# RG-LRU scan with mixture of experts on one core: all zero fills in a new fixed order of the main part, and the experts one after the other

## The chip, the cores and the metric

The kernel runs on one core of one Trainium2 chip. The metric is the device time of one execution in microseconds, the median of three runs. Five instruction queues work side by side: TensorE (PE, with its weight loads as PEld), VectorE (DVE), ScalarE (ACT), GpSimd (POOL), and SyncE (SP), which in this kernel does nothing but issue DMA transfers. Each queue runs its instructions in order. The instruction at its head waits until what it needs has been signalled.

## What is computed

```python
a_t = exp(8 * sigmoid(r_gate) * log(clip(sigmoid(a_param))))   # decay, per token and channel
u_t = sqrt(max(1 - a_t**2, 1e-6)) * sigmoid(i_gate) * x
h_t = a_t * h_(t-1) + u_t          # scan over 5056 tokens, 4 sequences, 256 channels
logits = h @ w_gate                # 20224 tokens, 8 experts
out = 0                            # (20224, 256)
for e in range(8):                 # at most 80 tokens of each expert, those of highest gate
    out[tok] = gate[tok] * (relu(h[tok] @ w1[e]) @ w2[e])
```

All but some 640 of the 20224 rows of the output are zero. They have to be written all the same, 20.7 MB; the three inputs are 62.1 MB together and the experts' weights 16.8 MB.

## The kernel before

**Main part** (lines 32 to 287). The 20224 tokens are cut into 22 units. Unit 0 and unit 1 are halves of 512 tokens, units 2 to 19 have 1024 tokens, unit 20 has 512 and unit 21 has 256. The order of all instructions of this part is written out by hand in the string ORDER, and each word of it becomes instructions on one queue. For unit u:

- `ru@s`, `iu@s`, `xu@s`: SP issues the load of r_gate, i_gate or x into slot s of the big tile Y (1 MB for a full unit)
- `Tu`: ACT takes tanh of r (line 117). `Au.h`: PE transposes it for channel half h (line 123). `Eu.h`: ACT takes exp and writes the decay into the state slot of the unit (line 126)
- `Qu`: POOL squares the decay (line 129). `Su.m`: ACT takes the square root for units u to u+m-1 (line 133); this needs another function table than tanh and exp, so every S group has a table load ahead of it and one behind it
- `Iu`: ACT takes tanh of i (line 137). `Uu`: POOL multiplies by x (line 140)
- `Bu.h`: PE transposes and adds (lines 147 and 148). `Nu.h`: DVE multiplies by the root (line 151). `Yu.h`: DVE scans (line 161)
- `lu`: PE computes the logits (line 237). `cs.k`: step k of the selection for chain s of units. `t`: an early search for the largest gates (line 272)
- `Z`: SP writes zeros to rows of the output. As long as no decay of the last pair (units 20 and 21) has been issued, one Z is one wide fill of 512 tokens (line 209, 0.5 MB in packets of 4 KB). After that, one Z is two narrow fills of 256 tokens (line 215, 0.25 MB each, packets of 1 KB)

The zeros of a wide fill are read from the state slot of the last pair, `Y[:, 19, 0]`. `E20.0` writes the first decay of unit 20 into the same place, so it can't start before every wide fill has been done.

Slots are shared. A load waits on SP until the last reader of what stood in its slot is done, and everything behind it on SP waits too. State slot p is free for streams until pair p gets its state, so there are fewer slots for streams towards the end.

**Selection** (lines 290 to 445). SP issues the weights of experts 0 and 1 (lines 300 and 303) and then `FILLS` = 11 narrow fills. DVE, POOL, ACT and PE find the 80 tokens of each expert. `keep_warm` (line 348) issues 13 and then 10 matmuls that nobody reads. `front` (line 514) fetches the column numbers of experts 0 and 1 into registers (`fetch`, line 497) and copies those columns of the state into XG (`copies`, lines 505 and 506): 32 by ACT, 24 by POOL and 24 by DVE for each expert.

**Experts** (line 531). The six fills that are left are issued first. For each expert, `first` is the product with w1 in two halves of 32 matmuls (line 546), `relu` empties a half (ACT half 0, DVE half 1), `second` is the product with w2 in two halves of 32 (line 556), `take` (ACT), `turn` (PE), `weigh` (DVE) and `scatter` (POOL, an indirect DMA) bring the result out. Weights have two buffers: w1 of expert e+2 is loaded when `first(e, 1)` is done, w2 of e+2 by halves when `second(e, half)` is done. The loop is staggered: the two halves of `first(k+1)` stand between the halves of `second(k)`.

Of the kernel before, what the change touches and what calls it, by code (L numbers as in the profile page):

```python
# [36 lines left out]
i8@13 N4.1 T8 B5.0 x8@18 E7.0 N5.0 I6 A7.1 Y4.1 i9@11 l3 E7.1 U6 Y5.0 T9 A8.0 B5.1 E8.0 i10@20 N5.1 I7 A8.1 Q7 Z B6.0 r11@17 Y5.1 E8.1 T10
A9.0 N6.0 U7 l4 E9.0 Y6.0 I8 A9.1 B6.1 c0.1 E9.1 Q8 B7.0 r12@24 N6.1 S7.2 x9@16 x10@12 Y6.1 l5 U8 c0.2 A10.0 N7.0 B7.1 Y7.0 E10.0 x11@22 Z
Q9 N7.1 I9 A10.1 i11@15 B8.0 Y7.1 E10.1 l6 T11 Q10 N8.0 c0.3 T12 A11.0 Y8.0 B8.1 c0.4 U9 E11.0 c0.5 r13@18 I10 i12@13 A11.1 N8.1 l7 E11.1
c0.6 r14@23 B9.0 Q11 S9.3 Y8.1 c0.7 A12.0 B9.1 N9.0 U10 c0.8 l8 Y9.0 i13@16 N9.1 I11 B10.0 x12@21 Y9.1 E12.0 U11 N10.0 T13 A12.1 c1.1 B10.1  # L40
Y10.0 E12.1 r15@20 I12 A13.0 Q12 Z N10.1 B11.0 E13.0 x13@14 Y10.1 c1.2 T14 A13.1 U12 N11.0 B11.1 I13 Y11.0 l9 E13.1 i14@22 x14@15 T15 N11.1
Q13 B12.0 c1.3 i15@17 S12.2 l10 Y11.1 U13 B12.1 N12.0 Y12.0 A14.0 r16@21 Z c1.4 I14 N12.1 B13.0 x15@24 Y12.1 E14.0 U14 I15 A14.1 N13.0
B13.1 E14.1 Y13.0 T16 i16@16 A15.0 Q14 l11 N13.1 E15.0 B14.0 c1.5 x16@18 S14.1 Z U15 Y13.1 A15.1 N14.0 B14.1 E15.1 Y14.0 r17@22 I16 Q15
A16.0 Z l12 N14.1 E16.0 B15.0 i17@23 Y14.1 S15.1 Z U16 A16.1 c1.6 B15.1 N15.0 l13 r18@24 E16.1 Y15.0 x17@17 T17 Q16 c1.7 Z N15.1 I17 A17.0
# [592 lines left out]
```

## Time and profile before

| what | value |
|---|---|
| median of 3 runs | 304.96 us (304.64 to 305.4) |
| the profiled execution, its own time | 304.55 us |
| its span, first to last instruction | 302.8 us |
| time outside the span in that execution | 1.75 us |
| busy share of the span: PE, DVE, ACT, POOL | 77%, 69%, 75%, 67% |
| moved by DMA | 100.95 MB, 333 GB/s over the span |
| mean granted clock of TensorE | 0.928 of full speed |

The time is the span and a constant around it. A busy share is an average over parts with different limits, so the tables by stretches are read first, then the timelines of single engines. "DMA share" in a stretch is the mean busy share of the 16 DMA engines; it can come out a little above 1. Releasers of waits are inferred from semaphores.

### The profile page before, as it was taken

Reading aid. Unit: us, or ns where it says so; the run is one execution under the profiler, and the core shown is the slowest. Engines: PE = TensorE matmul, PEld = TensorE weight load, DVE = VectorE, ACT = ScalarE, POOL = GpSimd, SP = SyncE. Lnnn points to the kernel's source line nnn. Section 1 sums busy time; section 2 is a strip of 40 time slices with the busy share of each in tenths; the row PEclk is TensorE's granted clock in tenths of the full one; section 3 lists DMA queues with packets and bytes.
Section 4 is the critical chain, followed back from the end, with each engine's and each line's share of the span. In section 5 each row is a group of like instructions: output and inputs, shape, how many; then the busy total and the mean of one; then the engine's idle time right before and its main releaser. Section 6 shows DMA issues by size and latency. Waiting matters only on the chain.

```text
span 302.8 us, 9258 instructions
## 1 busy us (share of the span) xinstructions
PE 231.9 (77%) x3422; PEld 204.9 (68%) x3422; DVE 209.5 (69%) x435; ACT 226.7 (75%) x441; POOL 202.2 (67%) x289
## 2 busy tenths in 40 slices
PE   1466489989989979979887976736739858999972
PEld 0355488878978878868776965635517658888761
...
GB/s 232 410 409 409 411 350 384 394 411 371 323 398 351 351 355 233 417 379 309 293 416 412 251 327 418 337 228 368 346 309 378 373 193 179 353 375 353 357 138 32
DMA packets 42436, 100.95 MB, mean 333 GB/s; under 512 B 3216, under 2 KB 22544, under 8 KB 42384
## 3 DMA queue, kind: packets, MB, share of 16 engines
...
HBM read 78.91 MB, written 21.36 MB: 331 GB/s over the span
## 4 chain that ended last, share of the span: by engine, by line
PE 13%; issue 11%; ACT 10%; DMA 10%; POOL 6%; DVE 6%; SPq 3%; POOLq 2%; ACTq 1%; DVEq 0%
DMA Y<-in_i_gate_dram 6%; POOL Y L506 3%; PE pd L348 3%; DMA Y<-in_r_gate_dram 3%; SPq L215 3%; ACT Y L505 3%; PE pu L147 2%; PE pu L148 2%; DVE Y L161 2%; ACT Y L133 2%; POOLq L499 2%; POOL Y L140 2%; ACT Y L126 1%; PE po L556 1%; ACT L133 1%
## 5 line engine op out<-in xcount | busy, mean ns | idle before, releaser
L140 POOL TENSOR_TENSOR Y<-Y 128x2048 f32<-128x2048 f32 (+2 forms) x22 | 90.7, 4122 | 27.2 <-ACT Y L137 18.0
L161 DVE TENSOR_TENSOR_SCAN Y<-Y,pu 128x1024 f32<-128x1024 f32 (+8 forms) x50 | 93.2, 1881 | 0.8
L129 POOL TENSOR_TENSOR Y<-Y 128x2048 f32<-128x2048 f32 (+2 forms) x22 | 71.6, 3258 | 21.2 <-ACT Y L126 12.6
L147 PE MATMUL pu<-ident,Y 128*128 128x128 f32 x316 | 78.3, 290 | 9.6 <-DVE Y L161 8.3
L151 DVE SCALAR_TENSOR_TENSOR pu<-Y,pu 128x1024 f32<-128x1024 f32 (+2 forms) x44 | 48.4, 1109 | 46.8 <-ACT Y L133 39.2
L148 PE MATMUL pu<-ident,Y 128*128 128x128 f32 x316 | 76.9, 287 | 5.0 <-POOL Y L140 4.9
L123 PE MATMUL pr<-ident,Y 128*128 128x128 f32 x316 | 51.3, 311 | 32.7 <-ACT Y L126 23.2
L123 PEld LDWEIGHTS pr<-ident,Y 128*128 128x128 f32 x316 | 40.5, 159 | 40.7 <-ACT Y L126 30.4
L126 ACT ACTIVATE Y<-pr,tiny 128x1024 f32<-128x1024 f32 (+2 forms) x44 | 49.0, 1113 | 14.7 <-PE pr L123 8.8
L147 PEld LDWEIGHTS pu<-ident,Y 128*128 128x128 f32 x316 | 47.2, 149 | 14.0 <-DVE Y L161 9.8
L148 PEld LDWEIGHTS pu<-ident,Y 128*128 128x128 f32 x316 | 47.2, 149 | 6.8 <-POOL Y L140 6.6
L137 ACT ACTIVATE Y<-Y 128x2048 f32<-128x2048 f32 (+2 forms) x22 | 38.1, 1733 | 3.6 <-DMA Y<-in_i_gate_dram 3.6
L237 PE MATMUL pl<-Y 128*32 128x64 f32 (+2 forms) x1344 | 39.2, 280 | 0.8 <-DVE Y L161 0.8
L117 ACT ACTIVATE Y<-Y 128x2048 f32<-128x2048 f32 (+2 forms) x22 | 38.0, 1731 | 0.7 <-DMA Y<-in_r_gate_dram 0.7
L133 ACT ACTIVATE Y<-Y 128x2048 f32<-128x2048 f32 (+2 forms) x22 | 37.3, 1733 | 1.2 <-POOL Y L129 1.1
L237 PEld LDWEIGHTS pl<-Y 128*32 128x32 f32 x1344 | 33.8, 125 | 4.5 <-issue 3.3
L505 ACT COPY Y<-Y 128x2 f32 x256 | 25.7, 192 | 12.5 <-POOL Y L506 7.6
L506 POOL COPY Y<-Y 128x2 f32 x192 | 24.6, 196 | 14.0 <-issue 7.2
L546 PE MATMUL ph<-Y 128*64 128x80 f32 x512 | 25.1, 249 | 8.5 <-ACT Y L505 5.3
L546 PEld LDWEIGHTS ph<-Y 128*64 128x64 f32 x512 | 22.3, 149 | 10.2 <-issue 5.6
L506 DVE COPY Y<-Y 128x2 f32 x192 | 20.9, 179 | 7.9 <-issue 7.9
L556 PE MATMUL po<-rows,Y 128*64 128x80 f32 x512 | 22.4, 241 | 0.0
...
## 6 DMA issues: line engine op xcount, KB each, us to landing
...
```

The lines of the kernel that those rows point to most:

```text
L123: nc.tensor.transpose(pr[:, c0:min(n, g + 512):nb], rr[:, at:at + P], ident)
L126: nc.scalar.activation(state(u, h), prs.pop((u, h))[:, :UNITS[u][2]], AF.Exp, scale=L[:, h:h + 1], bias=L[:, h:h + 1])
L129: nc.gpsimd.tensor_tensor(halves('r', u), a, a, op=ALU.mult)
L133: nc.scalar.activation(q, q, AF.Sqrt, scale=-0.25, bias=0.25)
L140: nc.gpsimd.tensor_tensor(i, i, flat('x', u), op=ALU.mult)
L147: nc.tensor.matmul(cols, xx[:, at:at + P], ident, start=True, stop=False, is_transpose=True)
L148: nc.tensor.matmul(cols, ii[:, at:at + P], ident, start=False, stop=True, is_transpose=True)
L151: nc.vector.scalar_tensor_tensor(pu, halves('r', u)[:, h], 0.5e-3, pu, op0=ALU.max, op1=ALU.mult)
L161: nc.vector.tensor_tensor_scan(y[:, s0:s1], y[:, s0:s1], q[:, s0:s1], init, op0=ALU.mult, op1=ALU.add)
L237: nc.tensor.matmul(pl[32 * j:32 * j + 32, s % 2, c0:c0 + n // NR], gates(h, b), Y[:, p, h, o + 4 * j + b:o + n:NR], start=(b == 0 and h == ...
L506: else: eng.tensor_copy(dst, src)
L546: nc.tensor.matmul(ph[j:j + P // 2, c % (FC // 2)], w1v(e)[:, h, c * P + j:c * P + j + P // 2], XG[:, e % 4, h], start=(h == 0), stop=(h = ...
```

## The change

1. `FILLS` and the two calls of `zero_fill` with it are gone. ORDER has 39 Z instead of 31: 23 wide fills (18 before) and 16 pairs of narrow ones (13 before), which is 78 of the 79 pieces of 256 tokens; one narrow fill follows behind the weights of experts 0 and 1. Before, 17 narrow fills followed there.
2. ORDER is new. The streams of the first and of the last units go to other slots and stand in another order. There are 11 S groups instead of 12.
3. `WARM` goes from (13, 10) to (13, 19).
4. The experts' loop runs expert by expert: both halves of `first`, then both halves of `second`.

```diff
-WARM = (13, 10)
+WARM = (13, 19)
-FILLS = 11
...
-r0@20 r1@20 r2@21 r3@22 T0 i0@23 A0.0 x0@24 w E0.0 T1 A0.1 r4@18 E0.1 T2 Q0 A1.0 i1@23 E1.0 r5@17 A1.1 E1.1 T3 A2.0 x1@24 E2.0 i2@16 I0
-A2.1 U0 E2.1 x2@15 I1 A3.0 Q1 B0.0 E3.0 i3@14 T4 A3.1 Q2 x3@13 E3.1 T5 A4.0 Q3 r6@12 E4.0 I2 A4.1 i4@11 B0.1 U1 E4.1 S0.4 r7@10 U2 N0.0
...
-c2.4 S17.1 c2.5 B17.1 U18 c2.6 A18.0 i19@23 Z c2.7 l16 N17.0 Z Z E18.0 N17.1 Z T19 c2.8 A18.1 c3.1 x19@22 Y17.0 c3.2 E18.1 I19 Z Q18 c3.3
-B18.0 Y17.1 c3.4 A19.0 S18.1 c3.5 B18.1 c3.6 l17 r20@20 N18.0 Z U19 Z E19.0 c3.7 N18.1 A19.1 Y18.0 i20@24 r21@20 E19.1 Z Z T20 c3.8 Q19
-Y18.1 A20.0 B19.0 E20.0 S19.1 t B19.1 A20.1 x20@22 Z Z x21@22 T21 Z E20.1 i21@24 Z I20 Q20 A21.0 l18 N19.0 E21.0 Z N19.1 U20 A21.1 E21.1 Z
-Y19.0 Z Q21 S20.2 Y19.1 B20.0 Z Z I21 N20.0 B20.1 U21 c4.1 Y20.0 c4.2 Z l19 N20.1 Z c4.3 B21.0 Y20.1 c4.4 Z c4.5 B21.1 l20 N21.0 Z N21.1
...
+r0@20 i0@21 r1@20 r2@22 r3@23 T0 A0.0 x0@24 w E0.0 T1 A0.1 i1@21 E0.1 r4@18 I0 Q0 A1.0 E1.0 T2 A1.1 i2@17 E1.1 T3 Q1 A2.0 x1@24 i3@16 E2.0
+U0 I1 A2.1 E2.1 x2@15 B0.0 T4 Q2 A3.0 B0.1 i4@14 E3.0 I2 A3.1 U1 x3@13 E3.1 Q3 S0.4 A4.0 r5@12 N0.0 N0.1 x4@11 U2 Y0.0 Y0.1 B1.0 r6@10 N1.0
...
+Y16.1 B17.0 c2.5 B17.1 c2.6 A18.0 I18 i19@23 N17.0 Z c2.7 l16 Z Z E18.0 U18 Y17.0 T19 A18.1 c3.1 c2.8 E18.1 N17.1 c3.2 I19 c3.3 Q18 x19@20
+B18.0 Z Y17.1 Z c3.4 Z S18.1 c3.5 B18.1 c3.6 U19 r20@24 r21@24 N18.0 c3.7 A19.0 N18.1 E19.0 Y18.0 x20@22 A19.1 Z x21@22 E19.1 Z Z c3.8
+B19.0 Z Y18.1 T20 Q19 T21 A20.0 E20.0 t B19.1 S19.1 A20.1 i20@20 l17 i21@20 Z Z Z Z E20.1 Q20 A21.0 N19.0 Z E21.0 I20 A21.1 N19.1 l18 Z I21
+U20 Y19.0 E21.1 Z Q21 S20.2 Z Y19.1 B20.0 U21 Z N20.0 Z c4.1 Y20.0 c4.2 B20.1 Z c4.3 B21.0 N20.1 l19 c4.4 Z N21.0 Y20.1 Z c4.5 B21.1 l20
...
-    zero_fill(FILLS)
+    zero_fill(-(-N // ZERO_TOKENS))
...
-        for k in 'APV': fetch(k, 0); copies(k, 0)
+        for k in 'APV': fetch(k, 0)
+        for k in 'APV': copies(k, 0)
...
-        nz[0] = filled
-        zero_fill(-(-N // ZERO_TOKENS))
...
-        first(0, 0); relu(0, 0); first(0, 1)
         for k in range(E):
-            e1, e2 = (k + 1 if k + 1 < E else None), (k + 2 if k + 2 < E else None)
-            if e2 is not None:
-                for q in 'APV': fetch(q, e2)
-            relu(k, 1)
-            if k >= 1: take(k - 1)
-            if e2 is not None:
-                copies('A', e2, 0, nA // 2); copies('P', e2); copies('V', e2)
-            if e1 is not None: first(e1, 0)
-            if k >= 1: turn(k - 1)
-            second(k, 0)
-            if e1 is not None: relu(e1, 0)
-            if e2 is not None: copies('A', e2, nA // 2)
-            if e1 is not None: first(e1, 1)
-            if k >= 1: weigh(k - 1); scatter(k - 1)
-            second(k, 1)
+            g = k + 2
+            if k: take(k - 1)
+            if 0 < k < E - 1: copies('A', g - 1, 16, 24)
+            first(k, 0); relu(k, 0)
+            if 0 < k < E - 1: copies('A', g - 1, 24); copies('V', g - 1, 20)
+            first(k, 1); relu(k, 1)
+            if k: turn(k - 1); weigh(k - 1)
+            if g < E:
+                for q in 'APV': fetch(q, g)
+                copies('A', g, 0, 16); copies('V', g, 0, 20); copies('P', g)
+            if k: scatter(k - 1)
+            second(k, 0); second(k, 1)
```

## Rows read from the trace of the kernel before

**Rows 1.** Timeline of SP from 188 us: start, duration, line, what it issues, count.
```profile
188.84 0.95 SPq L209 DMA_DIRECT2D out_dram<-Y  x2
...
204.55 15.44 SPq L215 DMA_DIRECT2D out_dram<-Y  x20
220.10 1.21 SPq L300 DMA_DIRECT2D Y<-in_moe_w_dram  x2
```

**Rows 2.** Stretches: busy time and instructions of each engine, granted clock, DMA share, GB/s.
```profile
0.00:220.00 220.00, 170.04 (x2310) 150.82 (x2310) 167.15 (x171) 191.32 (x144) 162.99 (x66) 0.95 0.95 355
4.00:44.00 40.00, 23.25 (x104) 20.02 (x105) 5.90 (x11) 33.78 (x27) 23.59 (x8) 0.87 1.03 409
72.00:128.00 56.00, 51.36 (x767) 46.20 (x766) 51.99 (x46) 55.33 (x38) 54.91 (x15) 1.00 0.93 345
128.00:152.00 24.00, 20.94 (x273) 18.87 (x272) 22.87 (x20) 23.49 (x18) 22.40 (x6) 1.00 0.97 331
164.00:181.00 17.00, 13.71 (x204) 12.59 (x205) 16.06 (x20) 14.71 (x11) 14.12 (x4) 0.90 0.87 303
181.00:195.00 14.00, 8.90 (x112) 7.76 (x111) 12.23 (x15) 10.01 (x8) 8.41 (x4) 0.85 1.02 415
```

**Rows 3.** Waits of ACT from 4 to 34 us: total, times, longest.
```profile
ACT Y L126 <- PE pr L123: 5.9, 8, 1.2
```

**Rows 4.** Wide fills issued from 128 to 152 us: count, duration of the issue, first and last start.
```profile
L209 SPq DMA_DIRECT2D out_dram<-Y x4: 455/459/754, 129.3 to 148.2; - x4
```

**Rows 5.** Timeline around 190 us: POOL U19, PE A20.0, ACT E20.0; idle before in brackets.
```profile
188.75 4.51 POOL L140 TENSOR_TENSOR Y<-Y 128x2048 f32<-128x2048 f32 x1 [3.14 <-DMA Y<-in_x_dram]
...
192.54 1.11 PE L123 MATMUL pr<-ident,Y 128*128 128x128 f32 x4 [2.24 <-ACT Y L117]
...
198.30 0.78 ACT L126 ACTIVATE Y<-pr,tiny 128x512 f32<-128x512 f32 x1 [5.81 <-PE pu L147]
```

**Rows 6.** Timeline of ACT at one S group: the table load and the root behind it.
```profile
139.71 1.28 ACT L133 ACT_TABLE_LOAD   x1
141.01 1.92 ACT L133 ACTIVATE Y<-Y 128x2048 f32<-128x2048 f32 x1
```

**Rows 7.** Timeline of the tail of the main part: T21, E20.1, I20, E21.1, S20.2, N20.0.
```profile
203.61 0.63 ACT L117 ACTIVATE Y<-Y 128x512 f32<-128x512 f32 x1
204.15 0.76 ACT L126 ACTIVATE Y<-pr,tiny 128x512 f32<-128x512 f32 x1
204.81 1.05 ACT L137 ACTIVATE Y<-Y 128x1024 f32<-128x1024 f32 x1
...
208.07 0.56 ACT L126 ACTIVATE Y<-pr,tiny 128x256 f32<-128x256 f32 x1 [1.76 <-PE pr L123]
...
209.95 1.58 ACT L133 ACTIVATE Y<-Y 128x1024 f32<-128x1024 f32 x2
...
211.04 0.70 DVE L151 SCALAR_TENSOR_TENSOR pu<-Y,pu 128x512 f32<-128x512 f32 x1 [1.86 <-PE pu L147]
```

**Rows 8.** Timeline of PE: keep_warm, first(0), second(0, 0), the last second.
```profile
237.24 4.58 PE L348 MATMUL pd<-Y,ident 128*128 128x256 f32 x20
244.97 4.08 PE L546 MATMUL ph<-Y 128*64 128x80 f32 x64 [3.15 <-ACT Y L505]
...
252.43 2.41 PE L556 MATMUL po<-rows,Y 128*64 128x80 f32 x32
...
294.20 2.44 PE L556 MATMUL po<-rows,Y 128*64 128x80 f32 x64
```

**Rows 9.** Timeline of ACT in the experts: relu(0, 0), then take(0) and take(1).
```profile
251.35 0.44 ACT L562 ACTIVATE rows<-ph 128x320 f32<-128x320 f32 x1 [0.29 <-issue]
...
258.51 0.29 ACT L563 COPY Y<-po 128x160 f32<-128x160 f32 x1 [1.54 <-DVE rows L561]
...
263.91 0.29 ACT L563 COPY Y<-po 128x160 f32<-128x160 f32 x1 [1.77 <-PE po L556]
```

**Rows 10.** Waits of PE from 244 to 303 us, of the first product for weights.
```profile
PE ph L546 <- DMA Y<-in_moe_w_dram: 1.6, 3, 0.7
```

More of the change, by code (lines that the diff above doesn't have):

```diff
@@ L32 @@
 ORDER = """
-r0@20 r1@20 r2@21 r3@22 T0 i0@23 A0.0 x0@24 w E0.0 T1 A0.1 r4@18 E0.1 T2 Q0 A1.0 i1@23 E1.0 r5@17 A1.1 E1.1 T3 A2.0 x1@24 E2.0 i2@16 I0
-A2.1 U0 E2.1 x2@15 I1 A3.0 Q1 B0.0 E3.0 i3@14 T4 A3.1 Q2 x3@13 E3.1 T5 A4.0 Q3 r6@12 E4.0 I2 A4.1 i4@11 B0.1 U1 E4.1 S0.4 r7@10 U2 N0.0
-N0.1 x4@9 Y0.0 Y0.1 B1.0 Q4 i5@8 A5.0 N1.0 B1.1 Y1.0 r8@23 I3 N1.1 B2.0 Y1.1 E5.0 U3 N2.0 x5@20 T6 A5.1 Y2.0 B2.1 E5.1 i6@24 N2.1 I4 A6.0
-Q5 B3.0 Y2.1 r9@21 E6.0 T7 A6.1 N3.0 U4 B3.1 x6@16 I5 Y3.0 l1 E6.1 i7@15 N3.1 Q6 S4.3 B4.0 Y3.1 x7@22 A7.0 l2 N4.0 U5 r10@14 Y4.0 B4.1
@@ L37 @@
[L37 to L44, printed above, removed]
@@ L45 @@
-B16.0 i18@20 Y15.1 S16.1 c1.8 B16.1 c2.1 U17 N16.0 l14 x18@18 E17.0 Y16.0 c2.2 T18 A17.1 l15 N16.1 E17.1 c2.3 B17.0 r19@21 I18 Q17 Z Y16.1
-c2.4 S17.1 c2.5 B17.1 U18 c2.6 A18.0 i19@23 Z c2.7 l16 N17.0 Z Z E18.0 N17.1 Z T19 c2.8 A18.1 c3.1 x19@22 Y17.0 c3.2 E18.1 I19 Z Q18 c3.3
-B18.0 Y17.1 c3.4 A19.0 S18.1 c3.5 B18.1 c3.6 l17 r20@20 N18.0 Z U19 Z E19.0 c3.7 N18.1 A19.1 Y18.0 i20@24 r21@20 E19.1 Z Z T20 c3.8 Q19
-Y18.1 A20.0 B19.0 E20.0 S19.1 t B19.1 A20.1 x20@22 Z Z x21@22 T21 Z E20.1 i21@24 Z I20 Q20 A21.0 l18 N19.0 E21.0 Z N19.1 U20 A21.1 E21.1 Z
@@ L49 @@
-Y19.0 Z Q21 S20.2 Y19.1 B20.0 Z Z I21 N20.0 B20.1 U21 c4.1 Y20.0 c4.2 Z l19 N20.1 Z c4.3 B21.0 Y20.1 c4.4 Z c4.5 B21.1 l20 N21.0 Z N21.1
-Y21.0 Y21.1 c4.6 l21 c4.7 c5.1 c4.8 c5.2 c5.3 c5.4 c5.5 c5.6 c5.7 c5.8
+r0@20 i0@21 r1@20 r2@22 r3@23 T0 A0.0 x0@24 w E0.0 T1 A0.1 i1@21 E0.1 r4@18 I0 Q0 A1.0 E1.0 T2 A1.1 i2@17 E1.1 T3 Q1 A2.0 x1@24 i3@16 E2.0
+U0 I1 A2.1 E2.1 x2@15 B0.0 T4 Q2 A3.0 B0.1 i4@14 E3.0 I2 A3.1 U1 x3@13 E3.1 Q3 S0.4 A4.0 r5@12 N0.0 N0.1 x4@11 U2 Y0.0 Y0.1 B1.0 r6@10 N1.0
+B1.1 Y1.0 E4.0 i5@21 N1.1 B2.0 Y1.1 T5 A4.1 N2.0 r7@20 E4.1 Y2.0 I3 Q4 A5.0 i6@24 B2.1 E5.0 N2.1 T6 A5.1 r8@17 U3 Y2.1 E5.1 i7@22 I4 A6.0
@@ new lines @@
+l1 E6.0 Q5 x5@15 T7 A6.1 B3.0 E6.1 x6@9 U4 B3.1 N3.0 I5 Y3.0 A7.0 Z T8 l2 r9@16 N3.1 E7.0 Q6 B4.0 S4.3 Y3.1 x7@23 A7.1 U5 B4.1 i8@13 N4.0
+l3 Y4.0 r10@14 N4.1 B5.0 E7.1 Y4.1 i9@18 I6 Q7 A8.0 N5.0 l4 x8@11 T9 Y5.0 B5.1 U6 I7 c0.1 x9@21 E8.0 N5.1 c0.2 I8 c0.3 A8.1 r11@15 Y5.1 U7
+B6.0 E8.1 x10@12 T10 A9.0 N6.0 B6.1 Y6.0 E9.0 Z Q8 c0.4 A9.1 I9 i10@24 l5 N6.1 E9.1 Y6.1 B7.0 Q9 S7.3 A10.0 c0.5 B7.1 N7.0 l6 U8 i11@22
+r12@23 Y7.0 N7.1 E10.0 U9 B8.0 r13@20 Y7.1 Z T11 A10.1 N8.0 B8.1 E10.1 c0.6 I10 Q10 A11.0 x11@13 Y8.0 Z l7 Z E11.0 N8.1 T12 A11.1 U10 B9.0
@@ new lines @@
+r14@17 Y8.1 E11.1 I11 A12.0 N9.0 c0.7 B9.1 E12.0 Y9.0 Q11 T13 A12.1 i12@21 i13@18 l8 N9.1 E12.1 x12@16 B10.0 c1.1 Q12 S10.3 Y9.1 A13.0
+B10.1 N10.0 U11 c0.8 l9 i14@24 Y10.0 N10.1 I12 B11.0 x13@14 Y10.1 Z Z E13.0 U12 T14 N11.0 A13.1 B11.1 Y11.0 E13.1 r15@22 I13 A14.0 Q13
+N11.1 B12.0 E14.0 x14@15 Y11.1 I14 A14.1 U13 c1.2 N12.0 B12.1 E14.1 c1.3 T15 l10 r16@21 N12.1 i15@16 Y12.0 c1.4 x15@23 A15.0 Q14 S13.2
+Y12.1 B13.0 Z U14 N13.0 B13.1 Y13.0 l11 i16@18 I15 N13.1 B14.0 E15.0 U15 r17@20 Y13.1 T16 A15.1 N14.0 B14.1 E15.1 c1.5 I16 A16.0 Q15 x16@24
@@ new lines @@
+Y14.0 Z l12 Z E16.0 S15.1 N14.1 B15.0 c1.6 i17@17 Z A16.1 U16 Y14.1 c1.7 E16.1 c2.1 B15.1 N15.0 T17 Y15.0 l13 Q16 x17@23 Z I17 A17.0 N15.1
+B16.0 E17.0 c1.8 r18@22 Y15.1 S16.1 Z A17.1 U17 c2.2 c2.3 B16.1 N16.0 l14 E17.1 x18@24 N16.1 i18@18 T18 Q17 Y16.0 r19@21 l15 c2.4 S17.1
+Y16.1 B17.0 c2.5 B17.1 c2.6 A18.0 I18 i19@23 N17.0 Z c2.7 l16 Z Z E18.0 U18 Y17.0 T19 A18.1 c3.1 c2.8 E18.1 N17.1 c3.2 I19 c3.3 Q18 x19@20
+B18.0 Z Y17.1 Z c3.4 Z S18.1 c3.5 B18.1 c3.6 U19 r20@24 r21@24 N18.0 c3.7 A19.0 N18.1 E19.0 Y18.0 x20@22 A19.1 Z x21@22 E19.1 Z Z c3.8
@@ L51 @@
+B19.0 Z Y18.1 T20 Q19 T21 A20.0 E20.0 t B19.1 S19.1 A20.1 i20@20 l17 i21@20 Z Z Z Z E20.1 Q20 A21.0 N19.0 Z E21.0 I20 A21.1 N19.1 l18 Z I21
+U20 Y19.0 E21.1 Z Q21 S20.2 Z Y19.1 B20.0 U21 Z N20.0 Z c4.1 Y20.0 c4.2 B20.1 Z c4.3 B21.0 N20.1 l19 c4.4 Z N21.0 Y20.1 Z c4.5 B21.1 l20
+N21.1 Z Y21.0 Y21.1 Z c4.6 l21 Z c4.7 c5.1 c4.8 c5.2 c5.3 c5.4 c5.5 c5.6 c5.7 c5.8
 """
@@ L529, in moe_kernel @@
     tstack.close()
-    filled = nz[0]
     def experts(own):
         ps_f = own.enter_context(tc.tile_pool(name="ps_f", bufs=1, space=bass.MemoryType.PSUM))
-        nz[0] = filled
-        zero_fill(-(-N // ZERO_TOKENS))
         hbuf = [rows[:, :FC * CAP], rows[:, FC * CAP:2 * FC * CAP]]
```

## The prediction

> **What bounds the kernel now.** I read the stretches first, then the timeline of SP, then ACT's and PE's. Until about 150 us ACT sets the pace of the main part: it is busy 55.33 of 56 us and 23.49 of 24 us [rows 2]. But the transfers are close behind, at a DMA share of 0.93 and 0.97 in the same stretches. The reader should compare the rates there. The loads of the start move 409 GB/s at a share of 1.03, the stretch from 181 us 415 at 1.02; the two long stretches from 72 to 152 us, with wide fills among the loads, move 345 and 331. At the end of the main part the transfers lead: U19 waits 3.14 us for x19, and E20.0 starts only at 198.30, after 5.81 us of idle ACT [rows 5]. The profile names PE there, but the transposes that E20.0 needs, A20.0, ended at 193.65 [rows 5]. What ended the wait I take to be the last wide fills, issued at 188.84 [rows 1]: zeros are read from where E20.0 writes. Behind the main part come the selection and the gather, which the change leaves alone, and the experts, where PE, ACT and the weights' transfers take turns.
>
> The profiled execution took 304.55 us; the median of the three runs is 0.41 above it, which I add at the end. About 0.3%, 0.9 us, is what a measurement of this kernel can tell from no change.
>
> **The start and the groups of roots.** In the first 34 us ACT's exps wait 5.9 us in eight places for PE's transposes [rows 3]. The new order puts I0, T2 and I1 into those gaps. The first stays, since nothing else is there yet, and it can be the longest, 1.2 us; with half a microsecond for the rest I take 4.0 us as gained, between 0 and 5.9. S0.4 then comes before T5 and E4, which is only an exchange on ACT. One S group less is two table loads less, 2 x 1.28 = 2.6 us; the root starts 0.02 us after its load [rows 6], so nothing hides behind the load. The Trainium skill (ScalarE: Activation LUTs, What ACT_TABLE_LOAD costs) puts a drain of 1.38 us beside each load, 2.66 us a switch. By that the group would be worth 5.3 us and the forecast 2.7 us lower; the trace shows no such gap, so I stay with 2.6. ACT could then be 6.6 us ahead.
>
> **Wide fills ahead of x19.** The new order has 16 wide fills ahead of x19, the old one 13. In clean company a wide fill costs its bytes, 0.524 MB / 415 GB/s = 1.3 us; two were issued at 188.84, within the stretch from 181 us that runs at 415 GB/s [rows 1, 2]. In 128 to 152 us four fills were issued, and at a share of 0.97 the rate should have been 415 x 0.97 / 1.02 = 395, not 331: 64 GB/s x 24 us = 1.5 MB are missing, 0.9 us a fill [rows 2, 4]. So the price is 1.3 to 2.2 us, and three cost 3.9 to 6.6. Against that stand the holes in the transfers: shares of 0.93, 0.97 and 0.87 against 1.02 over 56, 24 and 17 us are 5.0 + 1.2 + 2.6 = 8.8 us. All fills could fall into holes and cost nothing, or none. I take the middle price, 5.3 us, as paid out of the 6.6 us that ACT gains, so x19 lands 1.3 us sooner. The bounds are 6.6 us sooner and 6.6 later.
>
> **From x19 to E20.0.** Behind x19 the old queue holds five wide fills and r20, i20 and r21 (1.31 MB); the new one holds seven and r20, r21, x20 and x21 (1.57 MB). All must land before E20.0. At the clean price that is 2 x 1.27 + 0.26 / 0.415 = 2.5 + 0.6 = 3.1 us more. A part might be hidden by ACT's own path, but it already waits 5.81 us here, so I hide none. Together: E20.0 starts 3.1 - 1.3 = 1.8 us later, near 200.1.
>
> **The tail.** i20 and i21 now stand directly behind B19.1 on SP, where the old order had x20, x21 and i21 with six narrow fills among them. They land before I20 wants them, since E20.0, S19.1 and E20.1 take over 5 us. T21 moves ahead of E20.0, into ACT's wait, which saves its 0.6 us. S20.2 no longer stands behind an E21.1 that waits 1.76 us, but I21 (as long as T21) now comes ahead of it. From the end of E20.1 the root of unit 20 is done after E21.0 0.56, I20 1.05, I21 0.63, E21.1 0.56, a load 1.28 and its own 1.0: 5.1 us. N20.0 came 6.1 us after that end (211.04 - 204.91), with the root done 6.0 us after it [rows 7]. The next to be late is B20.0, which the row names, so I take 0.7 of the 0.9 us. DVE does the same work from there to the selection. The tail gains 1.3 us, between 0 and 2.
>
> **Fills, weights, gather.** Behind i21 there are 32 narrow fills on SP instead of 20 and then the first weights. At 15.44 / 20 = 0.77 us each that is 25 us, and the weights are issued near 225 instead of 220.10 [rows 1]; eight more issues follow. They are needed at first(0), near 245, so the delay is hidden by some 10 us of selection and gather. If that cover were gone, it would cost 5 us. The 17 fills that went from behind the weights were hidden too: nothing is gained there. Fetching for three engines before copying changes no engine's own order: 0. keep_warm runs 38 instead of 20 matmul passes of 4.58 / 20 = 0.229 us, 8.7 us in all, so first(0) starts at 245.9 instead of 244.97 but without the drop to half clock that makes its 64 matmuls 4.08 us instead of the 2.44 of the last 64 [rows 8]. Both ways it is over before relu(0, 0) at 251.35 [rows 9], which waits in ACT's queue behind the copies of expert 1: 0.
>
> **Experts.** PE now runs second(0, 0) where first(1, 0) stood: from 251.9, at half clock, 2.41 us as before [rows 8]. second(0, 1) and first(1) follow with three halves of 1.2 us, then turn and second(1), so first(2) starts near 261. From there ACT is the slower one while it gathers: take(0) to take(1) is 5.40 us [rows 9], in an iteration with its 32 copies, fetch and relu. Four such iterations reach 282.6. The last two experts need 4 x 1.22 + 0.4 = 5.3 us at most, so second(7, 1) ends near 292.9 instead of 294.20 + 2.44 = 296.6. The gain is 3.7 us. It comes from the weights: w1 of an expert is now asked for six halves ahead of its use instead of four, so the waits for it [rows 10] and the longer iterations around them go. The queue behind take on ACT is 8 copies and relu; second(k, 0) needs that relu and has first(k, 1) and turn to cover it. Without that cover it would cost some 0.5 us an expert. That is most of 3.7, so I bound the gain by 0 on one side; on the other, six experts at PE's 5.3 us would gain 0.4 more, and second(0) at full clock 1.2 more: 5.3 us.
>
> **Sum.** 304.55 + 1.8 - 1.3 - 3.7 = 301.4; with 0.41 the median is 301.8 us.
>
> **Rivals.**
>
> 1. *The wide fills make the main part wait for transfers* (slower). Before E20.0, 62.1 - 1.05 + 18 x 0.524 = 70.5 MB had to be moved, now 62.1 - 0.79 + 23 x 0.524 = 73.4 MB (what is subtracted are the last streams, which come after it). If the mean rate of the main part, 355 GB/s [rows 2], holds whatever ACT gains, E20.0 comes 2.9 / 0.355 = 8.1 us later. With the tail and the experts' gain: 304.96 + 8.1 - 1.3 - 3.7 = 308.1. It decides from the point at which E20.0 comes more than 5.0 us later (1.3 + 3.7), at 203.3. For it: E20.0 waits already. Against it: the stretches at 409 and 415 GB/s. The Trainium skill (DMA: Bandwidth & Descriptors, Where 436 GB/s comes from) names about 358 GB/s for HBM to one core as what binds; by that this rival would be sure. The two stretches here disagree with that as a limit.
> 2. *The fills fall into the holes*: x19 lands 6.6 us sooner, E20.0 starts at 194.8, and the sum is 304.96 - 6.6 + 3.1 - 1.3 - 3.7 = 296.5. For it: 8.8 us of holes.
> 3. *The experts gain nothing*, because ACT's chain of take, copies, relu and fetch paces them either way: 301.8 + 3.7 = 305.5, or 304.5 with a gain of one.
>
> **Chances.** The forecast 0.45, rival 1 0.26, rival 2 0.15, rival 3 0.14. Faster takes the forecast and rival 2, 0.60; rival 3 is mostly no change, 0.10, with 0.04 of it slower; slower is 0.30. The range goes from rival 2 to a little past rival 1 (x19 later by the dearer price): 296.5 to 309.5. The forecast's own range is 298.5 to 304, since the price of a fill and the experts' gain each move it by two or three us.
>
> **What would show it.** Right: fewer waits of exp on PE in the first 34 us; 22 table loads for the groups of the main part instead of 24; E20.0 at 198 to 202 with ACT idle before it; no wait of first(0) for weights; iterations of about 5.4 us from take to take and the last second ending 55.7 us after the start of keep_warm's second run, against 59.4 here (296.64 - 237.24). Wrong: E20.0 beyond 203; a DMA share of 1.0 with 350 GB/s or less and ACT idle from 130 to 180 us; PE waiting for ACT's relu between first and second; iterations no shorter than before.

## The result and the profile after

The changed kernel takes 301.33 us (median of 4 runs, 300.04 to 305.57), the kernel before beside it 305.18 us: a ratio of 0.9865, 95% interval 0.9833 to 0.9897. Two later comparisons gave 0.9916 (0.9869 to 0.9963) and 0.9889 (0.9829 to 0.9949). By these three ratios the change is worth 0.8 to 1.4%, 2.5 to 4.1 us; the forecast was 301.8 us. The total was right. Several of its terms were not, and this part of the document is mostly about that.

Executions spread over some 5 us, and the longest of them count in the medians but not in the ratios, so kernels are compared by the ratios. The profile shown below is of an execution of the changed kernel that took 302.54 us, with a span of 300.7 us. In the changed kernel the lines of the helpers stand one lower (wide fills L208, narrow fills L214, weights L299 and L302), `first` is L543, `second` L553, `copies` L504 and L505.

Stretches of the changed kernel (columns as in [rows 2]):

```profile
0.00:220.00 220.00, 169.25 (x2181) 153.04 (x2181) 163.37 (x162) 188.51 (x142) 162.86 (x66) 0.91 0.97 367
4.00:44.00 40.00, 24.10 (x144) 20.66 (x144) 12.26 (x16) 35.80 (x29) 23.83 (x9) 0.91 1.03 404
...
72.00:128.00 56.00, 50.11 (x668) 46.35 (x672) 50.84 (x44) 52.87 (x37) 52.05 (x14) 0.97 0.97 363
128.00:152.00 24.00, 21.47 (x302) 20.03 (x290) 20.29 (x18) 21.03 (x15) 19.24 (x5) 0.86 0.93 316
...
181.00:195.00 14.00, 9.86 (x60) 9.20 (x61) 12.64 (x14) 10.47 (x10) 11.03 (x5) 0.78 1.03 417
...
212.00:216.00 4.00, 2.96 (x14) 2.56 (x15) 2.31 (x5) 2.76 (x4) 2.21 (x3) 0.50 1.02 349
```

ACT is busier at the start (35.80 of 40 us, before 33.78 [rows 2]) and idler later (21.03 of 24 us from 128 us, before 23.49 [rows 2]). What it gained it gave back in front of late loads, as its timeline shows:

```profile
129.49 1.91 ACT L116 ACTIVATE Y<-Y 128x2048 f32<-128x2048 f32 x1 [2.46 <-DMA Y<-in_r_gate_dram]
...
158.91 1.91 ACT L136 ACTIVATE Y<-Y 128x2048 f32<-128x2048 f32 x1 [3.06 <-DMA Y<-in_i_gate_dram]
...
201.17 0.78 ACT L125 ACTIVATE Y<-pr,tiny 128x512 f32<-128x512 f32 x1 [6.06 <-DMA out_dram<-Y]
...
211.58 1.06 ACT L132 ACTIVATE Y<-Y 128x1024 f32<-128x1024 f32 x1
```

The third line is E20.0, 2.87 us later than in [rows 5]. The profile now says itself what ended the wait: a transfer that reads Y and writes the output, a wide fill. The prediction had taken that from the addresses. U19 on POOL still waits for x19, which lands 0.41 us sooner than in [rows 5]:

```profile
188.34 4.53 POOL L139 TENSOR_TENSOR Y<-Y 128x2048 f32<-128x2048 f32 x1 [2.97 <-DMA Y<-in_x_dram]
```

SP and then PE, where the gather and the experts begin:

```profile
189.96 2.33 SPq L208 DMA_DIRECT2D out_dram<-Y  x3
...
199.79 25.18 SPq L214 DMA_DIRECT2D out_dram<-Y  x32
225.08 1.13 SPq L299 DMA_DIRECT2D Y<-in_moe_w_dram  x2
...
252.15 0.82 SPq L299 DMA_DIRECT2D Y<-in_moe_w_dram  x2
```

```profile
241.41 8.47 PE L347 MATMUL pd<-Y,ident 128*128 128x256 f32 x38
249.81 2.44 PE L543 MATMUL ph<-Y 128*64 128x80 f32 x64
253.04 2.44 PE L553 MATMUL po<-rows,Y 128*64 128x80 f32 x64 [0.80 <-ACT rows L559]
...
276.38 2.08 PE L553 MATMUL po<-rows,Y 128*64 128x80 f32 x53 [1.35 <-issue]
...
292.50 2.44 PE L553 MATMUL po<-rows,Y 128*64 128x80 f32 x64
```

Four marks divide the 2.1 us between the two spans:

| mark | before | changed | difference | of it in this part |
|---|---|---|---|---|
| E20.0 starts [rows 5] | 198.30 | 201.17 | +2.87 | +2.87 |
| keep_warm's second run starts [rows 8] | 237.24 | 241.41 | +4.17 | +1.30 |
| second(0, 0) starts [rows 8] | 252.43 | 253.04 | +0.61 | -3.56 |
| the last second ends [rows 8] | 296.64 | 294.94 | -1.70 | -2.31 |
| span | 302.8 | 300.7 | -2.1 | -0.4 |

In this execution the main part, with the tail and the selection behind it, lost 4.2 us. All of the gain lies behind it, 5.9 us, and more than half of that lies in the gather, in a part that the prediction had put at nothing.

The two halves are not equally firm. Of the kernels below, three have the old order up to E20.0 (before_no_late, the new loop alone, loop and warm-up) and one has the whole of the new order (warm_split). With the two kernels here that makes these starts:

| profiles | E20.0 | keep_warm's second run |
|---|---|---|
| old order, four | 198.05 to 198.88, mean 198.5 | 237.24 to 238.38, mean 237.7 |
| new order, two | 199.70 and 201.17, mean 200.4 | 238.62 and 241.41, mean 240.0 |

So the loss ahead of keep_warm is 4.2 us in the profile shown and 2.3 in the mean, while the time from keep_warm to the end of the last second is 53.5 us in both profiles of the new order. 5.9 - 2.3 = 3.6 us fits the 2.5 to 4.1 of the ratios.

### The profile page after: what moved, and what is told of

Its sections match the earlier page's. It is cut to its first block, busy times and chain, and to the rows that moved or that the text cites. A ratio compares the mean times of both kernels' runs of the same rounds, so it can differ in the third digit from the quotient of the medians.

```text
span 303.8 us, 9276 instructions
## 1 busy us (share of the span) xinstructions
PE 235.1 (77%) x3440; PEld 210.1 (69%) x3440; DVE 210.2 (69%) x435; ACT 224.3 (74%) x439; POOL 202.4 (67%) x289
## 4 chain that ended last, share of the span: by engine, by line
PE 25%; ACT 21%; DMA 16%; DVE 12%; issue 11%; POOL 10%; SPq 3%; POOLq 1%; ACTq 0%; DVEq 0%
DMA Y<-in_i_gate_dram 9%; ACT Y L125 6%; PE pr L122 6%; ACT Y L136 5%; DVE Y L160 5%; ACT Y L116 4%; PE pu L146 4%; PE pu L147 4%; DMA Y<-in_r_gate_dram 4%; PE pd L347 3%; DMA out_dram<-Y 3%; PE ph L543 3%; ACT Y L132 3%; POOL Y L505 3%; POOL Y L139 3%
## 5 line engine op out<-in xcount | busy, mean ns | idle before, releaser
L146 PE MATMUL pu<-ident,Y 128*128 128x128 f32 x316 | 82.1, 298 | 7.8 <-DVE Y L160 5.2
L147 PE MATMUL pu<-ident,Y 128*128 128x128 f32 x316 | 80.7, 296 | 5.7 <-POOL Y L139 5.3
L122 PE MATMUL pr<-ident,Y 128*128 128x128 f32 x316 | 50.6, 308 | 36.2 <-ACT Y L125 27.9
L146 PEld LDWEIGHTS pu<-ident,Y 128*128 128x128 f32 x316 | 49.1, 156 | 11.9 <-DVE Y L160 5.5
L147 PEld LDWEIGHTS pu<-ident,Y 128*128 128x128 f32 x316 | 48.8, 154 | 7.8 <-POOL Y L139 7.8
L504 ACT COPY Y<-Y 128x2 f32 x256 | 26.5, 191 | 18.2 <-issue 10.0
L505 POOL COPY Y<-Y 128x2 f32 x192 | 24.3, 201 | 10.9 <-issue 7.3
L505 DVE COPY Y<-Y 128x2 f32 x192 | 22.6, 177 | 11.3 <-issue 11.3
L553 PE MATMUL po<-rows,Y 128*64 128x80 f32 x512 | 20.9, 235 | 4.3 <-issue 4.3
L553 PEld LDWEIGHTS po<-rows,Y 128*64 128x64 f32 x512 | 19.1, 137 | 6.2 <-issue 5.7
L543 PE MATMUL ph<-Y 128*64 128x80 f32 x512 | 19.7, 233 | 0.0
```

The lines of the kernel that those rows point to most:

```text
L122: nc.tensor.transpose(pr[:, c0:min(n, g + 512):nb], rr[:, at:at + P], ident)
L146: nc.tensor.matmul(cols, xx[:, at:at + P], ident, start=True, stop=False, is_transpose=True)
L147: nc.tensor.matmul(cols, ii[:, at:at + P], ident, start=False, stop=True, is_transpose=True)
L505: else: eng.tensor_copy(dst, src)
```

## Experiments

All are compared with runs of the kernel before on the same chip. "keep_warm" below is always its second run.

**The changed kernel again** (no edit), twice, as the base of two groups.

> The changed kernel as it is, for a profile beside the others. My theory (the main part ends about as before, the experts give the gain): E20.0 at 198 to 202, the last second ending about 55.7 us after the start of keep_warm's second run. The rival (the main part gives the gain, the experts none): E20.0 at 194 or 195 and 59 us from keep_warm to the last second.

> The changed kernel again, beside the next three on the same chip. If the main part is slower by the wide fills, as the last profiles show, E20.0 starts at 201 to 203 after more than 6 us of idle ACT, against 198.3 before. If it is not, E20.0 starts at or before 198.3.

Measured: 303.04 us, ratio 0.9916, and 302.50 us, ratio 0.9889. The intervals overlap with the first one, but the three medians lie 1.7 us apart. In the profile of the second, E20.0 starts at 201.17 us after 6.06 us of idle ACT, as expected. Differences under 1.5 us between kernels of different groups mean little here.

**The loop and the warm-up.** First the changed kernel with the staggered loop:

```diff
...
-            first(k, 0); relu(k, 0)
...
-            first(k, 1); relu(k, 1)
...
-            second(k, 0); second(k, 1)
...
+            if e1 is not None: first(e1, 0)
...
+            second(k, 0)
...
+            if e1 is not None: first(e1, 1)
...
+            second(k, 1)
...
```

> The new order, fills and keep_warm, with the staggered loop of the experts from before. My theory: slower than the changed kernel by 3.7 us, so about the time before or up to 2 us faster. The rival that the main part gives all: no difference to the changed kernel, 301.3.

Measured: ratio 1.0003 (0.9941 to 1.0066), where the changed kernel had 0.9916 (0.9869 to 0.9963) beside it. The difference is 0.9% or 2.7 us, uncertain by 2.4. Without its loop no gain of the change is left to see. Next the kernel before with the new loop alone, which is the same edit the other way round:

> The kernel before with only the experts' loop changed (WARM, ORDER and the 17 narrow fills behind the weights as before). My theory: 301.3 to 302, 3 to 4 us faster than before, since the rest of the change is worth about nothing. The rival that the main part gives all: 305.

Measured: 304.84 us, ratio 0.9974 (0.9926 to 1.0022). By these numbers the same loop gains less here than it seemed to be worth there (305 x 0.0026 = 0.8 us against 2.7, though each is uncertain by 1.5 us or more); the predicted gain was 3.7. PE shows a part of why:

```profile
237.34 4.58 PE L348 MATMUL pd<-Y,ident 128*128 128x256 f32 x20
245.45 3.90 PE L546 MATMUL ph<-Y 128*64 128x80 f32 x64 [3.53 <-ACT Y L505]
252.07 3.71 PE L556 MATMUL po<-rows,Y 128*64 128x80 f32 x64 [2.73 <-ACT rows L562]
```

PE stands idle for 3.53 and 2.73 us, and its first two products run mostly at half clock, 3.90 and 3.71 us where 2.44 is full speed. Only the second of these costs time: first(0) is over at 249.35, and second(0, 0) waits 2.73 us for ACT's relu all the same. Then the warm-up alone:

```diff
-WARM = (13, 19)
+WARM = (13, 10)
```

> The changed kernel with keep_warm at 10 again. My theory: no difference, 301.3, because relu(0, 0) waits behind the copies of expert 1 on ACT and both ways first(0) is over by then. Rival: 19 pays since first(0) and second(0) run at full clock, then this is 1 to 2 us slower. Third: 19 is too many and holds first(0) up, then this is 0.5 to 1.5 us faster.

Measured, in the changed kernel: 304.70 us, ratio 0.9952 (0.9898 to 1.0006) against 0.9916 for the changed kernel itself. That is 1.1 us, inside the error of the two. Then both together in the kernel before:

```diff
-WARM = (13, 10)
+WARM = (13, 19)
```

(on top of the new loop, in the kernel before)

> The kernel before with the new loop of the experts and with 19 passes in keep_warm's second run in place of 10; order, fills and the order of fetch and copies stay as before. Theory: the experts' gain needs the loop and the longer warm-up together, and the new order of the main part is worth about nothing by itself. Then this kernel is level with the changed one, near 302.5 us where the kernel before takes 306, ratio 0.985 to 0.993; second(0, 0) takes 2.4 us and not 3.71, and first(2) starts some 21 us after keep_warm's second run, not 23.6. Rival: the gain also needs the transfers to be over before the gather starts, as they are in the new order. Here they still run at 244 us and hold up the fetch of the slots (3.8 to 4.3 us from the slot list to the first copy, against 2.1), so that the ratio stays at 0.995 to 0.998, as with the loop alone.

Measured: 303.26 us, ratio 0.9927 (0.9882 to 0.9971), at the edge of the theory's range: 0.7% or 2.2 us, where the loop alone had 0.3%. The difference of the two, 1.4 us, is uncertain by 2.

```profile
237.91 8.47 PE L348 MATMUL pd<-Y,ident 128*128 128x256 f32 x38
246.31 2.44 PE L546 MATMUL ph<-Y 128*64 128x80 f32 x64
250.82 2.43 PE L556 MATMUL po<-rows,Y 128*64 128x80 f32 x64 [2.07 <-ACT rows L562]
```

Both products are at full clock now, and first(2) starts 20.1 us after keep_warm. From second(0, 0) to the end of the last second it is 42.24 us, 43.52 with the loop alone: 1.3 us, as much as second(0, 0) is shorter. second(0, 0) comes 12.9 us after the start of keep_warm, 14.7 with the loop alone, but still 1.3 later than the 11.6 of the changed kernel. Something in the gather is faster there that is neither loop nor warm-up.

**The fills at the end of the main part.** First the four wide fills between x20 and E20.0 are taken out of ORDER, then also the three behind x19. The rows are written all the same, by nine and fifteen narrow fills. Not all of these stand behind the first weights: the profiles show two of the nine at 191.17 us and six of the fifteen at 188.51, behind x21, so that seven and nine are left there. These early ones read another tile than E20.0 writes.

```diff
-... x20@22 A19.1 Z x21@22 E19.1 Z Z c3.8
-B19.0 Z Y18.1 T20 Q19 T21 A20.0 E20.0 ...
+... x20@22 A19.1 x21@22 E19.1 c3.8
+B19.0 Y18.1 T20 Q19 T21 A20.0 E20.0 ...
```

> The changed kernel without the four wide fills that stand between x20 and E20.0; their rows are written by eight narrow fills behind the weights of experts 0 and 1, where the transfers stand idle. Theory A (E20.0 waits for the last wide fills): the 6.4 us wait is gone or under 2 us, E20.0 starts near 197, the kernel is 3.5 to 5 us faster than the changed one. Theory B (another wait takes its place at once: i20, or Q19 for S19.1): E20.0 is earlier, the selection is not, and the time is within 1 us of the changed kernel's.

> As the one before, and without the three wide fills behind x19 as well. Theory A: nothing more is gained, within 1 us of the kernel with four taken out, since ACT no longer waits for fills there. Theory C (the fills also delay r20 and x20 and through them the tail): another 1 to 3 us faster.

Measured: 302.24 us, ratio 0.9879 (0.9821 to 0.9937), and 302.73 us, ratio 0.9896 (0.9829 to 0.9962): the same as the changed kernel beside them. But E20.0 moved by 5.66 us in the first, as its row shows, and by 7.34 us, to 193.83, in the second:

```profile
195.51 0.78 ACT L125 ACTIVATE Y<-pr,tiny 128x512 f32<-128x512 f32 x1 [0.75 <-PE pr L122]
```

So the fills did set the end of the main part, at 5.66 / 4 = 1.4 us each in these two executions. In warm_split and no_late_fills below, which differ up to E20.0 by the same four fills, it is 199.70 against 198.05, 0.4 us each. What E20.0 gained in the first kernel shrank behind it. N19.0, which needs S19.1 behind E20.0, is 1.67 us sooner than in the changed kernel (203.53 against 205.20), since DVE is busy with the early search `t` until then; keep_warm is 3.58 us sooner, and the last second ends 1.54 sooner. The time is theory B's, the wait, DVE's, is not one that it named. With all seven out E20.0 is only 1.7 us sooner still, since the wait before it is PE's now. The same kernel with 14 passes in place of 19:

> Four wide fills taken out, and keep_warm 14 instead of 19. Theory D (19 holds first(0) and with it the first weights of expert 2 up, and the weights set the pace from there): 1 to 3 us faster than with 19. Theory E (what counts is that PE keeps its clock until second(0)): the granted clock falls to half at second(0) again, and it is 1 to 2 us slower.

Measured: 302.50 us, ratio 0.9898 (0.9846 to 0.995), no different. Its profile shows two things. The first is how far two executions of the same code can come apart; the code of the two kernels is the same up to keep_warm's second run. The granted clock (last but two columns) in two stretches of the tail, first for four_out and then for this kernel:

```profile
204.00:208.00 4.00, 1.09 (x40) 0.84 (x32) 4.00 (x3) 3.76 (x6) 4.00 (x3) 0.50 1.06 363
208.00:212.00 4.00, 2.77 (x12) 2.37 (x13) 4.00 (x5) 1.33 (x2) 0.58 (x2) 0.50 1.05 352
```

```profile
204.00:208.00 4.00, 2.66 (x60) 2.05 (x50) 4.00 (x4) 3.75 (x6) 4.00 (x3) 0.82 1.04 350
208.00:212.00 4.00, 3.67 (x77) 3.08 (x77) 3.97 (x9) 1.62 (x3) 0.53 (x2) 1.00 1.04 343
```

E20.0 starts at 195.51 in the one and 195.52 in the other, keep_warm at 237.83 and 234.12. The clock is not all of these 3.7 us. DVE's search `t` and N19.0, in the same order:

```profile
195.50 1.20 DVE L271 MAX8 rows<-rows 128x8 f32<-128x1024 f32 x1
202.20 1.42 DVE L276 CAST tiny<-tiny 128x16 f32<-128x16 uint32 x1
203.53 2.35 DVE L150 SCALAR_TENSOR_TENSOR pu<-Y,pu 128x1024 f32<-128x1024 f32 x2
```

```profile
193.84 1.20 DVE L271 MAX8 rows<-rows 128x8 f32<-128x1024 f32 x1
200.54 0.18 DVE L276 CAST tiny<-tiny 128x16 f32<-128x16 uint32 x1
200.62 2.36 DVE L150 SCALAR_TENSOR_TENSOR pu<-Y,pu 128x1024 f32<-128x1024 f32 x2
```

DVE is 1.66 us late already before E20.0, and one CAST that took 1.42 us and not 0.18 makes it 2.91 at N19.0. At most the other 0.8 us can be the clock's behind N19.0.

The second thing is that what this execution had gained was lost in the gather:

```profile
234.12 6.31 PE L347 MATMUL pd<-Y,ident 128*128 128x256 f32 x28
244.09 4.54 PE L543 MATMUL ph<-Y 128*64 128x80 f32 x64 [3.66 <-ACT Y L504]
249.85 4.04 PE L553 MATMUL po<-rows,Y 128*64 128x80 f32 x64 [1.22 <-ACT rows L559]
```

Both products are at half clock, as theory E had it, but the kernel is no slower. keep_warm starts 3.7 us sooner than in four_out and second(0, 0) only 0.5 (250.36 there), for the reason that the next experiments show.

**The fetch of the slots.** DVE writes the list of slots, each engine fetches its share for expert 0 into registers and copies, and then the same for expert 1. DVE in the changed kernel and in the kernel before:

```profile
241.28 0.23 DVE L517 TENSOR_SCALAR lg<-pv 8x80 int32<-8x80 f32 x1 [0.40 <-PE pv L516]
243.63 2.80 DVE L505 COPY Y<-Y 128x2 f32 x24 [2.12 <-issue]
```

```profile
237.10 0.23 DVE L518 TENSOR_SCALAR lg<-pv 8x80 int32<-8x80 f32 x1 [0.40 <-PE pv L517]
241.16 2.83 DVE L506 COPY Y<-Y 128x2 f32 x24 [3.83 <-issue]
```

The gap is 2.12 us in the one and 3.83 us in the other. It is 2.92 in four_out, 4.02 in seven_out, 5.94 in four_out_warm14, 4.26 with the loop alone and 2.64 with loop and warm-up. What goes with it is the state of the transfers, here in the stretch from 240 to 244 us (share and GB/s in the last two columns), of the changed kernel and of the kernel before:

```profile
240.00:244.00 4.00, 3.60 (x30) 3.03 (x29) 0.95 (x7) 0.04 (x1) 0.36 (x3) 1.00 0.02 5
```

```profile
240.00:244.00 4.00, 1.82 (x9) 1.26 (x7) 2.84 (x25) 2.37 (x25) 2.86 (x23) 1.00 1.04 353
```

In the kernel before, the narrow fills behind the weights are still being written; in the changed kernel one such fill is left, and the transfers had ended when the list came.

second(0, 0) waits for ACT, which fetches and copies for two experts before relu(0, 0). So both of its fetches count (times in us; the second fetch is the gap between ACT's two runs of copies):

| kernel | list to ACT's first copy | ACT's second fetch | start of the list to second(0, 0) |
|---|---|---|---|
| before | 4.30 | 2.97 | 15.33 |
| loop alone | 4.69 | 2.71 | 14.87 |
| loop and warm-up | 3.29 | 2.28 | 13.04 |
| four_out | 3.34 | 1.84 | 12.66 |
| four_out_warm14 | 6.54 | 1.84 | 15.86 |
| changed | 2.45 | 1.84 | 11.76 |

The two fetches are 1.85 + 1.13 = 2.98 us shorter in the changed kernel than before, and that is most of the 3.56 us of the gather. The other 0.6 is that second(0, 0) follows relu(0, 0) at once and no longer stands behind first(1, 0). They also make the whole difference between the loop alone and loop with warm-up (1.40 + 0.43 of 1.83), and the first fetch that between four_out and four_out_warm14 (3.20 of 3.20): the list came 3.7 us sooner there, while the transfers still ran. That led to two kernels that leave these fills out:

```diff
-    zero_fill(-(-N // ZERO_TOKENS))
```

(in four_out: the nine narrow fills that were left for the end; in four_out seven of them stand behind the weights)

> four_out without the fills behind the first weights: the last seven narrow fills are left out, so these rows of the output are not zeroed. Theory: what four_out gains ahead of E20.0 (5.7 us) it loses to these fills, which run beside the fetch of the slots and in front of nothing else; without them 2.1 us pass from the slot list to the first copy (2.9 in four_out, 2.1 in the changed kernel), and the time falls by 1.5 us or more, to about 300.5. Rival: the gain is lost where PE's clock is at half in the tail, and in the experts, which wait longer for w2 when they start sooner; then the time stays within 0.7 us of four_out, near 302.

Measured: 298.21 us, ratio 0.9774 (0.9723 to 0.9825), against 0.9879 for four_out: 1.05%, 3.2 us, uncertain by 2.4. DVE's gap is 2.12 us, as expected. Not all of the 3.2 us is the fetch: from the list to second(0, 0) it is 11.76 us against 12.66, from there to the end 42.06 against 43.04, and 1.3 us are there already when the list is written. This kernel says that the fills cost time; it does not divide the time. The second does it where it counts, in the kernel before:

```diff
-    zero_fill(FILLS)
...
-        zero_fill(-(-N // ZERO_TOKENS))
```

> The kernel before without the 17 narrow fills behind the first weights (11 in the front, 6 at the head of the experts); these rows of the output are not zeroed. It tests the step of the prediction that put these fills at nothing. Theory: they are not hidden, they hold up the fetch of the slots. Without them 2.1 us pass from the slot list to DVE's first copy (3.83 in the kernel before), second(0, 0) starts 1.7 us sooner after keep_warm's second run (15.2 us in the kernel before), and the time falls by about 1.7 us, ratio 0.990 to 0.997. Rival: they are hidden behind the gather, as the prediction had it; then the time stays within 0.3%, ratio 0.997 to 1.003, and first(0) or relu(0, 0) takes up what the fetch gains. The main part up to E20.0 is the same in both.

Measured: 302.69 us, ratio 0.9888 (0.984 to 0.9937): 3.4 us, between 1.9 and 4.9, more than the theory had, and the rival is out. PE, then ACT, and both in the kernel before:

```profile
238.38 4.58 PE L347 MATMUL pd<-Y,ident 128*128 128x256 f32 x20
244.26 2.44 PE L544 MATMUL ph<-Y 128*64 128x80 f32 x64 [1.30 <-ACT Y L504]
249.34 1.33 PE L544 MATMUL ph<-Y 128*64 128x80 f32 x32 [2.64 <-ACT Y L504]
250.46 1.31 PE L554 MATMUL po<-rows,Y 128*64 128x80 f32 x32
```

```profile
240.93 3.13 ACT L504 COPY Y<-Y 128x2 f32 x32 [6.44 <-POOL Y L505]
245.91 3.33 ACT L504 COPY Y<-Y 128x2 f32 x32 [1.85 <-PE ph L544]
```

```profile
241.63 3.13 ACT L505 COPY Y<-Y 128x2 f32 x32 [7.59 <-POOL Y L506]
247.73 3.33 ACT L505 COPY Y<-Y 128x2 f32 x32 [2.97 <-PE ph L546]
251.16 1.54 PE L546 MATMUL ph<-Y 128*64 128x80 f32 x32 [2.12 <-ACT Y L505]
```

DVE's gap is 2.13 us, 1.7 less than before. second(0, 0) starts 12.08 us after keep_warm against 15.19: 3.1 us. ACT's first fetch is 1.85 us shorter (2.45 and not 4.30) and its second 1.12 (1.85 and not 2.97), so 2.97 of the 3.1 us are the two fetches; the theory had counted one. PE idles 1.30 us behind keep_warm and not 3.15, and its first 64 matmuls run at full clock, 2.44 us and not 4.08 [rows 8]. But behind them first(1, 0) waits for ACT's copies of expert 1 in both kernels, 2.64 and 2.12 us, so this is not where the time comes from. From second(0, 0) to the end nothing is gained (44.54 us, 44.21 before).

**An earlier first(0).** In the changed kernel first(0) has its data near 247 us and starts at 249.81, behind keep_warm. Some of the passes were put behind it:

```diff
-WARM = (13, 19)
+WARM = (13, 14)
...
+            if k == 0: keep_warm(6, ps_f)
             second(k, 0); second(k, 1)
```

> The changed kernel with 14 passes in keep_warm's second run in place of 19, and 6 more passes between first(0, 1) and second(0, 0). Theory: the transfers of the weights pace the experts, and the first of them that is not there ahead (w1 of expert 2) can be asked for only when first(0) is over. first(0) has its data by 247 us in the changed kernel and starts at 249.8, behind keep_warm; here it starts about 2.2 us sooner, w1 of expert 2 is issued 2.2 us sooner, and the waits for w2 in the later experts (0.6, 1.35 and 0.67 us) shrink: 1 to 2.5 us less than the changed kernel, 300 to 301.5 where that takes 302.5. Rival 1: the copies on ACT, relu(0, 0) behind them and second(0, 0) set the pace, and nothing is gained: 302.5. Rival 2: PE's clock falls between keep_warm and second(0, 0) all the same, and it costs 1 to 2 us: 303.5 to 304.5.

Measured: 301.11 us, ratio 0.9894 (0.9846 to 0.9942), as the changed kernel (0.9889).

```profile
238.62 6.31 PE L347 MATMUL pd<-Y,ident 128*128 128x256 f32 x28
244.86 2.44 PE L543 MATMUL ph<-Y 128*64 128x80 f32 x64
247.22 2.86 PE L347 MATMUL pd<-Y,ident 128*128 128x256 f32 x12
250.25 2.43 PE L553 MATMUL po<-rows,Y 128*64 128x80 f32 x64 [0.17 <-ACT rows L559]
```

first(0) starts 6.24 us after keep_warm and not 8.40, and w1 of expert 2 is asked for 2.2 us sooner. second(0, 0) starts 11.63 us after keep_warm in both, since it waits for relu(0, 0) behind ACT's copies, and from there to the end it takes 41.91 us against 41.90. Rival 1 holds: nothing that comes before relu(0, 0) shortens the experts. Why is not shown; it fits that second(0, 0) is what gives back the first buffer of w2. None of the kernels here that write all rows is measurably faster than the changed one.

## Why the prediction came out right

The total came out by luck in part: what lies ahead of keep_warm and what lies behind it were missed in opposite directions by about as much. The steps of the prediction, with the changed kernel's profile unless another run is named:

- **The start, 4.0 us: right in kind, too large.** ACT's waits for PE from 4 to 34 us are 2.9 us in four places instead of 5.9 in eight [rows 3]. In the mean of all profiles they are 3.1 us with the new order and 5.4 with the old: 2.3 us gained.
- **One S group less, 2.6 us: as stated.** There are 11 loads ahead of roots in place of 12, and 24 in all in place of 26, at 1.28 us each. No run did this part alone.
- **Three more wide fills ahead of x19, 5.3 us: dearer than they were.** x19 lands at 188.34 us, 188.75 before. In the six profiles with the new order up to x19 it lands at 186.33 to 189.13, 187.6 in the mean, in the four with the old one at 188.47 to 189.00, 188.7: 1.1 us sooner, where 1.3 had been forecast. Of 2.3 + 2.6 = 4.9 us gained that leaves 3.8 paid, 1.3 us a fill, the clean price, if the gains reach x19 in full; no run separates them. The start taken too high and the fills too dear cancel.
- **From x19 to E20.0, 3.1 us: as stated.** It is 201.17 - 188.34 = 12.83 us here and 13.37 in warm_split, 9.55 before [rows 5] and 9.5 to 10.3 in the other profiles of the old order: 3.3 us more in the mean. Together E20.0 is 1.9 us late in the mean, 1.8 forecast, and 2.9 late in the profile shown, short of rival 1's 5.0.
- **Rival 1's rule.** The stretches at the start and from 181 us still move 404 and 417 GB/s, and the mean to 220 us rose from 355 to 367 [rows 2]. A fixed mean rate, which rival 1 needs, is not what happens. The Trainium skill (Perfetto Trace Analysis, Roofline) says that a core alone can pull more than its share of 358 GB/s, up to about 435; the rows agree with that, and not with 358 as a limit.
- **The tail, 1.3 us: right for the root, not for what follows.** From E20.0 to the root of unit 20 it is 10.41 us against 11.65 [rows 5, 7], 1.2 us less. But N20.0 on DVE starts at 213.71, after 1.66 us of waiting for PE's B20.0, and that is 12.54 us after E20.0 against 12.74: only 0.2 us less. From E20.0 to keep_warm it is 1.3 us more. PE's granted clock is 0.50 from 212 to 216 us, the lower of its two levels (1.2 of 2.4 GHz), where it was 1.00 before. The prediction named B20.0 as the next to be late and still counted 0.7 of 0.9 us as gained; "DVE does the same work from there" left out that PE's transposes stand between DVE's steps. In warm_split, the same code, it is 38.92 us from E20.0 to keep_warm; in the four profiles of the old order it is 38.9 to 39.5. So the loss of 1.3 us belongs to the execution and not surely to the change, but a gain is not there either.
- **Fills behind the weights, 0: the step that failed.** "The 17 fills that went from behind the weights were hidden too: nothing is gained there." They were not hidden. before_no_late prices them at 3.4 us (1.9 to 4.9), of which 3.0 are ACT's two fetches. They run beside the fetches, and the time in which weights are not needed yet is not time in which a transfer costs nothing. The prediction had asked only whether the weights would be late.
- **WARM, 0: right for first(0), not for second(0, 0).** 19 passes hold the clock until the first products, as stated. first(0) at half clock is covered by relu(0, 0), as stated too. second(0, 0) is not: with the new loop alone it loses 1.3 us to half clock, and it gets them back with 19 passes. The prediction had left it at half clock in the sum and kept the 1.2 us for its bound.
- **The experts, 3.7 us: too large.** From second(0, 0) to the end the changed kernel takes 41.90 us, 44.21 before: 2.3 us, and 1.2 of them are the clock of second(0, 0) (2.41 us for its first half in [rows 8], 1.2 at full clock). With the new loop alone it is 43.52, 0.7 us less than before. The pace is not ACT's 5.40 us from take to take. From first(2) at 260.37 to first(7) at 289.72 an expert takes 29.35 / 5 = 5.9 us, PE waits in the middle of second (0.61, 1.35 and 0.67 us) and the transfers run at a share of 1.04 and 368 GB/s from 257 to 288 us. At that rate an expert's 2.1 MB of weights take 5.7 us, near the 5.9, so the weights' transfers pace the experts as far as these numbers show; that PE's waits are for w2 is inferred, the profile names no releaser. The check given, 55.7 us from keep_warm to the last second, came out at 53.5, since it holds the 3.6 us of the gather that had been put at 0.

So the errors have opposite signs: 2.2 us too little expected of what lies behind keep_warm (5.9 gained against 3.7), and 1.8 too much of what lies ahead of it, most of that in the tail (2.3 lost in the mean of the profiles, 0.5 by the forecast).

What stays open: which part of the fetch waits while transfers run, and whether the new order without its fills is worth anything, since no run had the one without the other. The gains of the late fills (3.4) and of loop and warm-up (2.2), each measured in the kernel before, add up to about the 5.9 us behind keep_warm; what the change gives is less by the loss ahead of it. Every mark is read from one execution of a kernel, and keep_warm's start differs by 2.8 us between two executions of the same code.
